# Attention, a feed-forward layer and routed experts in one kernel: another first expert, fewer static rows, a count in place of a flush, one state step

## The chip, the cores and the metric

The kernel runs on 1 core of one Trainium2 chip. The metric is the device time of one execution in microseconds (us), the median of several runs. The inputs are those of the reference below; weights w_in and w_out of the second layer arrive as 64-bit floats, all else as 32-bit floats.

## The reference

Three layers follow one another on 4 x 768 = 3072 tokens.

```python
# 1: linear attention with decay, 8 heads of 48
for t in range(S):
    cur = np.einsum('bhd,bhe->bhde', u[None] * kt, vt)
    y[:, :, t] = np.einsum('bhd,bhde->bhe', rt, state + cur)
    state = w[None, :, :, None] * state + np.einsum('bhd,bhe->bhde', kt, vt)
# 2: 384 -> 1024 -> 384
h = x @ w_in
e = np.exp(h - h_max); sm = e / (np.sum(e, axis=-1, keepdims=True) + 1e-09)
solu = h * sm
ln = (solu - mu) / np.sqrt(var + 1e-06) * g_ln
x = ln @ w_out
# 3: each token goes to one of 8 experts
expert_idx = np.argmax(x @ w_gate, axis=1)
for e in range(E):
    mask = expert_idx == e
    h = np.maximum(x[mask] @ w1[e], 0.0)
    out[mask] = gate_w[mask, None] * (h @ w2[e])
```

## The kernel before, in words

**Tiles and stages.** Tokens go in 24 tiles of 128. Layer 1 runs a chunked form: a tile is one chunk of 128 steps, six tiles make a sequence, and a state of 48 x 48 for each head is carried from tile to tile. `update` (line 433) computes what a tile adds to the state, for two heads at a time, so that PSUM holds 128 x 96 blocks of which only the two diagonal quarters are wanted; `advance` (lines 437 to 444) writes these two quarters, partitions 0 to 63 and 64 to 127, into `state`, with one VectorE instruction each, adding the decayed state `sdec` (line 447, `state` times `wdec`; `wdec` is zero off the diagonal quarters). Layer 2 is `mm1` (line 474), the softmax and norm (lines 480 to 526), and `mm2` (line 559), whose last columns are the gate. Routing is `choose`, `rank`, `place` and `send` (lines 566 to 616): each token gets a row in the DRAM table `xs`, 3072 rows for each expert, by the running counts `cum`. Layer 3 reads the rows of one expert after another back (`gather`, line 739), turns them (`etrans`, 753), and multiplies with w1 (`emm1`, 772) and w2 (`emm2t`, 815, where the expert has more than 384 rows, else `emm2`, 797, in tiles of 128 rows). Every f32 product is three products of split parts (high by high, high by low, low by high).

**Static rows.** An expert's count is known only on the chip, while its matmuls have fixed sizes: `CAPS` gives the rows of the first expert, and of the others in falling order of their counts. Rows beyond the count hold a token number that the scatter at the end leaves out. In the kernel before the first expert is always expert 0, with 480 rows, in two parts of 256 and 224 that can start before the last tiles are routed. After the last tile `count` and `sort` (lines 632 to 642) order the other seven by count, and `who` (line 648) loads the number of each as a register of SyncE, by which its weights and rows are addressed. `judge` (line 662 on) raises a flag when a count is over its static rows or a guard on the inputs fails; then a general path computes everything again.

**Weights.** w_in comes in three pieces of 128 x 1024, w_out in four of 128 x 768. `to_f32` (line 158) turns the two words of each 64-bit number into one 32-bit float: ScalarE takes the absolute value of the high word (line 167), VectorE flushes numbers under a bound to zero (line 169) and puts the bits together in three instructions (172, 174, 176). `win_hi`, `win_lo` (188, 191) and `wout_g`, `wout_max`, `wout_hi`, `wout_lo` (202 to 253) follow. Products of `mm1` need all of w_in, those of `mm2` all of w_out.

**What sets the order.** Every step is an `op` with an engine, a cost, what it comes after, and a priority `first`, worked out from the constants `X`. `plan` (line 1057 on) goes through the steps as a list scheduler: of those that could start within `X["EPS"]` of the earliest, the one with the lowest priority is next. The result is the program order on every engine, SyncE's DMA queue and GpSimd's queue among them. Some steps (`either`) go to VectorE or GpSimd, whichever the plan finds free first. The changed lines of the plan are in `conv` (873), the steps of layer 1 (931 on), `count` and `sort`, and the loop over the experts (about 980 on).

Of the kernel before, what the change touches and what calls it, by code (L numbers as in the profile page):

```python
# [8 lines left out]
F32 = mybir.dt.float32  # L9
F32R = mybir.dt.float32r  # L10
I32 = mybir.dt.int32
F16 = mybir.dt.float16
# [18 lines left out]
CAPS = (CAP, 480, 448, 432, 416, 400, 384, 368)  # L31
# [9 lines left out]
def body(ctx, tc, r, k, v, w, u, w_in, w_out, g_ln, w_gate, w1, w2, out):  # L41
# [18 lines left out]
    def sml(name, slot=None):  # L60
# [25 lines left out]
    X = dict(ET=-429.78, GG=-233.7, SO=-294.91, FL=-505.75, OL=1, ybuf=10, tmp=1, rkv=3, LAT=0.06, SELF=0.05,  # L86
             PRE=1.4, EPS=0.06, TA=144.7, TB=237.7, TM=276.51, NA=8, NB=9, M0=1038.64, W0=81.15, TW=251.26,
             W1=-298.48, TV=171.34, PF=134.77, PW=224.32, F0=466.45, EL=3, e=3, S0=12.3, P0=10.1, D0=2.5,
             L0=140.96, L1=105.03, U0=108.15, KG=5.83, PT=2, ZT=-610.22, F2=261, TE=288.64, GA=-152.99,
             GW=-226.57, GN=-97.54, DB=-0.71, KS=5.09, K0=202.89, K1=-109.3, xtrans=-983.06, kev=-515.9,  # L90
             ahi=-247.51, vlo=-135.95, ruk=1202.87, attend=-89.6, choose=-323.29, xhi=-244.14, vhi=27.84,
             own=138.51, hvar=-317, hmax=-289.95, gexp=-194.8, ktrans=655.01, rtrans=830.4, hexp=357.44,
             ztrans=-337.98, asum=-344.06, rev=-225.55, xlo=-713.89, decay=439.69, alo=897.3, rank=107.2,
             ld=344.13, xrow=-508.46, mm2=767.79, causal=-1488.31, hseed=638.5, send=114.58, hsolu=83.6,
             yout=-62.13, zlo=360.17, scores=-213.79, square=539.99, place=100.24, ysquare=-70.93,
             advance=-563.07, update=-90.68, zscale=-828, hroot=-416.04, mm1=19.74, aval=-17.98, kpow=98.58)
# [36 lines left out]
    G.memset(state, 0.0)  # L133

# [23 lines left out]
    def to_f32(t, n, is64, dst):  # L158

        dst.append(t[:, 0:n])  # L160
        if is64:
# [21 lines left out]
    def win_bits(c):  # L183
        raw["f", c] = f = []
        return to_f32(raw.pop(("i", c)), FF, w_in.dtype != F32, f)
# [10 lines left out]
    def wout_bits(c):  # L196
        raw["g", c] = f = []
        return to_f32(raw.pop(("o", c)), 2 * DM, w_out.dtype != F32, f)
# [56 lines left out]
    def fold_all():  # L255

        fold_load()
        for c in range(KD):
            win_load(c)
            run(win_bits, c)  # L260
            win_hi(c)
            win_lo(c)
        for c in range(0, KF, 2):
            wout_load(c)
            run(wout_bits, c)
# [13 lines left out]
    def tables():  # L279
# [4 lines left out]
        V.tensor_copy(wbad, wc)  # L284
        V.tensor_scalar(wc, wc, WLO, WHI, op0=ALU.max, op1=ALU.min)
        V.tensor_tensor(wbad, wbad, wc, op=ALU.not_equal)
# [342 lines left out]
    for e in range(1, E):  # L629
        V.memset(kcap[:, e:e + 1], 8.0 * CAPS[e] + 7)  # L630
# [704 lines left out]
```

## Time and profile before

| what | us |
|---|---|
| median of 3 runs | 634.06 |
| the runs | 633.23 to 634.15 |
| the profiled execution, its own time | 634.09 |
| its span, first to last instruction | 632.4 |
| PE (matmul) busy in the span | 578.8 |
| DVE (VectorE) busy | 455.9 |
| ACT (ScalarE) busy | 347.9 |
| POOL (GpSimd) busy | 272.0 |

The profile is that of one execution. Engines are PE for TensorE's matmuls, PEld for its weight loads, DVE, ACT, POOL and SP (SyncE, which issues most DMAs). Start times are counted from the first instruction. A group of instructions is named by its line, its engine, its operation, and what it writes and reads; "x24" is a count. A share of busy time over the whole span is a mean over stages that differ, so the stages are read one by one.

### The profile page before, as it was taken

The numbers are of one execution on the slowest core, as the hardware profiler recorded it, in microseconds if no ns is written. First come the engines' busy times: TensorE is split into PE (matmuls) and PEld (weight loads), VectorE is DVE, ScalarE is ACT, GpSimd is POOL, SyncE is SP. The second block draws the span as 40 slices with busy tenths as digits, with TensorE's granted clock in tenths as the row PEclk, the third lists the DMA queues.
The fourth block names the chain that finished last, engine by engine and source line by source line (L and its number), as shares of the span: only waits on it lengthen the run. The fifth ranks groups of instructions, "written<-read, shape, count | busy, mean of one in ns | idle before, by whom it ended". The sixth has DMA issues, their size and how long they took to land.

```text
span 632.4 us, 10941 instructions
## 1 busy us (share of the span) xinstructions
PE 578.8 (92%) x4037; PEld 497.1 (79%) x4037; DVE 455.9 (72%) x799; ACT 347.9 (55%) x577; POOL 272.0 (43%) x435
## 2 busy tenths in 40 slices
PE   2767887999999999999999989999999999999992
PEld 2667776867777777778877648998889999999992
DVE  7999989998798888888875655447665767578010
ACT  2754557379777676777756753445252535345210
POOL 3778767746755865665535452110001021001211
PEclk9876978999999999999999989999999999999997
DMA  9943736994565592947044624735455675764110
GB/s 170 227 109 60 157 93 198 238 160 93 99 116 95 106 129 54 154 72 129 28 76 98 196 100 163 273 107 189 129 182 161 200 203 170 208 141 108 52 38 23
DMA packets 163185, 83.79 MB, mean 132 GB/s; under 512 B 140100, under 2 KB 156346, under 8 KB 162736
## 3 DMA queue, kind: packets, MB, share of 16 engines
q1 hardware_dynamic: 159808, 73.51, 51.7%
q0 software_dynamic: 3312, 9.47, 4.5%
q8 instruction: 34, 0.56, 0.4%
q14 instruction: 31, 0.25, 0.1%
HBM read 51.71 MB, written 16.30 MB: 108 GB/s over the span
## 4 chain that ended last, share of the span: by engine, by line
PE 52%; DVE 17%; issue 10%; DMA 10%; POOL 4%; ACT 4%; POOLq 0%; SPq 0%; ACTq 0%; DVEq 0%
PE emm L772 12%; PE mm L559 10%; PE mm L474 9%; DMA out<-o,gt 8%; PE emm L815 7%; PE emm L797 3%; PE scores L396 2%; PE update L433 2%; DVE AT L400 2%; PE attend L419 2%; DVE tmp L169 2%; DVE tmp L174 2%; PE etrans L753 1%; DVE vl L369 1%; PE attend L422 1%
## 5 line engine op out<-in xcount | busy, mean ns | idle before, releaser
L847 POOL DMA_INDIRECT out<-o,gt x30 | 30.1, 1003 | 206.8 <-ACT o L843 104.3
L559 PE MATMUL mm<-wo,zT 128*128 128x392 f16 x576 | 100.7, 332 | 0.5 <-DVE zT L550 0.4
L474 PE MATMUL mm<-wi,xh 128*128 128x512 f32 x288 | 91.8, 400 | 3.3 <-DVE AT L400 3.3
L559 PEld LDWEIGHTS <-zT 128*128 128x128 f16 x576 | 55.9, 98 | 38.4 <-issue 1.3
L783 ACT ACTIVATE hh<-emm 128x896 fp32r<-128x896 f32 (+7 forms) x32 | 28.2, 882 | 82.3 <-PE emm L772 79.6
L786 DVE SCALAR_TENSOR_TENSOR hl<-emm,hh 128x896 fp32r<-128x896 f32 (+7 forms) x32 | 33.4, 1044 | 55.2 <-ACT hh L783 55.2
L772 PE MATMUL emm<-exh,w1h 128*128 128x256 f32 (+8 forms) x216 | 73.1, 338 | 0.0
L772 PE MATMUL emm<-exh,w1l 128*128 128x256 f32 (+8 forms) x216 | 72.6, 336 | 0.0
L772 PE MATMUL emm<-exl,w1h 128*128 128x256 f32 (+8 forms) x216 | 72.6, 336 | 0.0
L474 PEld LDWEIGHTS mm<-wi,xh 128*128 128x128 f32 x288 | 52.7, 189 | 13.6 <-DVE AT L400 3.7
L474 PE MATMUL mm<-wi,xl 128*128 128x512 f32 x144 | 56.5, 392 | 0.0
L815 PE MATMUL emm<-hh,w2h 128*128 128x480 f32 (+4 forms) x120 | 43.8, 365 | 0.0
L815 PE MATMUL emm<-hh,w2l 128*128 128x480 f32 (+4 forms) x120 | 43.1, 359 | 0.0
L815 PE MATMUL emm<-hl,w2h 128*128 128x480 f32 (+4 forms) x120 | 43.1, 359 | 0.0
L613 POOL DMA_INDIRECT xs<-row,pos x24 | 29.7, 1236 | 30.0 <-issue 13.8
L396 PE MATMUL scores<-rT,kT 64*128 64x128 f32 x384 | 32.5, 317 | 11.0 <-DVE st L494 7.7
L772 PEld LDWEIGHTS emm<-exh,w1l 128*128 128x128 f32 x216 | 40.7, 189 | 1.4
L772 PEld LDWEIGHTS emm<-exh,w1h 128*128 128x128 f32 x216 | 40.8, 189 | 1.4
L772 PEld LDWEIGHTS emm<-exl,w1h 128*128 128x128 f32 x216 | 40.8, 189 | 1.3
L396 PEld LDWEIGHTS scores<-rT,kT 64*128 64x128 f32 x384 | 27.4, 216 | 15.4 <-issue 7.0
L500 ACT ACTIVATE z<-e,st 128x1024 f16<-128x1024 f32 x24 | 27.5, 1145 | 18.0 <-DVE st L494 11.0
L480 DVE TENSOR_REDUCE st<-mm 128x1 f32<-128x1024 f32 x24 | 29.3, 1220 | 10.6 <-PE mm L474 9.2
(208 smaller groups left out, 1566.0 us busy)
## 6 DMA issues: line engine op xcount, KB each, us to landing
stage<-in_moe_w SPq DMA_DIRECT2D x16, 768.0 KB, 4.8
stage<-in_moe_w SPq DMA_DIRECT2D x8, 1024.0 KB, 5.0
xs<-zf SPq DMA_DIRECT2D x8, 772.0 KB, 12.2
rkv<-in_r SPq DMA_DIRECT2D x24, 192.0 KB, 4.9
rkv<-in_k SPq DMA_DIRECT2D x24, 192.0 KB, 5.1
rkv<-in_v SPq DMA_DIRECT2D x24, 192.0 KB, 4.5
stage<-in_moe_w SPq DMA_DIRECT2D x8, 512.0 KB, 4.2
xg<-xs SPq DMA_DIRECT2D x5, 772.0 KB, 6.4
```

The lines of the kernel that those rows point to most:

```text
L396: T.matmul(ps[:, a, j * P:(j + 1) * P], kT[h, j, :], rT[h, j, :], start=True, stop=True)
L474: T.matmul(ps[:, n, :], a[:, j, :], wi[b][:, j, n * 512:(n + 1) * 512], start=(j == 0 and m == 0), stop=(j == KD - 1 and m == 2))
L480: V.tensor_reduce(st[:, 0:1], tk["h", i], op=ALU.max, axis=AX.X, negate=True)
L500: A.activation(z[:, 0, :], tk["e", i], AF.Square, scale=-float(FF), bias=st[:, 2:3], accum_out=st[:, 4:5])
L559: T.matmul(ps[:, 0:OW], zz[:, a, c, :], wo[b][:, c, :], start=(c == 0 and m == 0), stop=(c == KF - 1 and m == 2))
L613: G.indirect_dma_start(out=xs, out_offset=bass.IndirectOffsetOnAxis(ap=pos.bitcast(U32), axis=0), in_=row, in_offset=None, bounds_check=E ...
L772: T.matmul(ps[:, x, :], a[:, j, fc * P:(fc + 1) * P], b[:, j, :], start=(j == 0 and m == 0), stop=(j == KD - 1 and m == 2))
L783: A.activation(cols(d, "hh", q), d["pm", q], AF.Relu)
L786: V.scalar_tensor_tensor(cols(d, "hl", q), d.pop(("pm", q)), 0.0, cols(d, "hh", q).bitcast(F32), op0=ALU.max, op1=ALU.subtract)
L797: T.matmul(ps[0:n, 0:DM], a[:, c, j * P:j * P + n], b[:, c, :], start=(c == 0 and m == 0), stop=(c == KF - 1 and m == 2))
L815: T.matmul(ps[:, 0:d["nr"]], a[:, c, m * P:(m + 1) * P], b[:, c, :], start=(c == 0 and x == 0), stop=(c == KF - 1 and x == 2))
L847: G.indirect_dma_start(out=out, out_offset=bass.IndirectOffsetOnAxis(ap=d["gt"][0:n, j, 1:2].bitcast(U32), axis=0), in_=d.pop(("o", j))[0: ...
```

## The change

1. The first expert is chosen on the chip: after tile 14 (`PK`) a matmul counts, `sort` and `leader` find the expert with the highest count, and `who(0)` loads its number on SyncE. Its weights and its gather wait for that. The sort at the end puts it first by adding 1e6 to its key.
2. `CAPS` falls for the other seven: 120 rows fewer in all. `judge` checks the first expert by its mask `first8`.
3. `to_f32` flushes nothing any more. ScalarE computes, after the absolute value, how far each word lies below the bound, and sums that into a column of `wbad`; any such word raises the flag. VectorE's three bit instructions read the high words in place.
4. `advance` writes the whole 128 x 384 block with one instruction. The off-diagonal quarters of `state` now hold numbers, and `wdec` makes them zero in `sdec`.
5. The constants `X` of the plan are others, and the costs of the changed steps in the plan too.

```diff
-CAPS = (CAP, 480, 448, 432, 416, 400, 384, 368)
+CAPS = (CAP, 464, 432, 416, 400, 384, 368, 344)
...
-    X = dict(ET=-429.78, GG=-233.7, SO=-294.91, FL=-505.75, OL=1, ybuf=10, tmp=1, rkv=3, LAT=0.06, SELF=0.05,
-             PRE=1.4, EPS=0.06, TA=144.7, TB=237.7, TM=276.51, NA=8, NB=9, M0=1038.64, W0=81.15, TW=251.26,
...
+    X = dict(PK=14, ET=-29.23, GG=-120.46, SO=-383.87, FL=374.6, OL=1, ybuf=10, tmp=1, rkv=3, LAT=0.06,
+             SELF=0.05, PRE=1.4, EPS=0.1, TA=176.56, TB=248.64, TM=254.17, NA=8, NB=9, M0=495.42, W0=42.93,
...
-    cuma = const.tile([P, 1], F16, name="cuma")
+    cuma = const.tile([P, E], F16, name="cuma")
...
-    wbad = const.tile([P, 4], F32, name="wbad")
+    wbad = const.tile([P, 12], F32, name="wbad")
+    thr = const.tile([P, 1], F32, name="thr")
...
+    G.memset(wbad, 0.0)
+    G.memset(thr, 1.125 * 2.0 ** -15)
...
             A.activation(hm.bitcast(F32), hi.bitcast(F32), AF.Abs)
             yield
-            V.scalar_tensor_tensor(hm.bitcast(F32), hm.bitcast(F32), 1.125 * 2.0 ** -15, hi.bitcast(F32),
-                                   op0=ALU.is_ge, op1=ALU.mult)
+            if small is None:
+                V.scalar_tensor_tensor(hm.bitcast(F32), hm.bitcast(F32), 1.125 * 2.0 ** -15, hi.bitcast(F32),
+                                       op0=ALU.is_ge, op1=ALU.mult)
+                hi = hm
+            else:
+                A.activation(hm.bitcast(F32), hm.bitcast(F32), AF.Relu, scale=-1.0, bias=thr, accum_out=small)
             yield
-            V.tensor_scalar(a, hm, 3, 0x3FFFFFF8, op0=ALU.logical_shift_left, op1=ALU.bitwise_and)
+            V.tensor_scalar(a, hi, 3, 0x3FFFFFF8, op0=ALU.logical_shift_left, op1=ALU.bitwise_and)
             yield
-            V.scalar_tensor_tensor(a, hm, -0x40000000, a, op0=ALU.bitwise_and, op1=ALU.bitwise_or)
+            V.scalar_tensor_tensor(a, hi, -0x40000000, a, op0=ALU.bitwise_and, op1=ALU.bitwise_or)
...
     def advance(i):
-        p4 = tk.pop(("pu", i))[:, 0:DM].rearrange("p (j a d) -> p j a d", j=4, a=2)
-        for a in range(2):
-            h = slice(64 * a, 64 * a + 64)
-            if i % NC == 0:
-                V.tensor_scalar(state[h, :, a, :], p4[h, :, a, :], SV, None, op0=ALU.mult)
-            else:
-                V.scalar_tensor_tensor(state[h, :, a, :], p4[h, :, a, :], SV, sdec[h, :, a, :], op0=ALU.mult, op1=ALU.add)
+
+        flat, ps = state.rearrange("p j a d -> p (j a d)"), tk.pop(("pu", i))[:, 0:DM]
+        if i % NC == 0:
+            V.tensor_scalar(flat, ps, SV, None, op0=ALU.mult)
+        else:
+            V.scalar_tensor_tensor(flat, ps, SV, sdec.rearrange("p j a d -> p (j a d)"), op0=ALU.mult, op1=ALU.add)
...
+    def leader():
+
+        V.tensor_scalar(first8, iota8, lead[:, 0:1], None, op0=ALU.is_equal)
+        yield
+        V.scalar_tensor_tensor(koff, first8, 1e6, koff, op0=ALU.mult, op1=ALU.add)
...
     def who(e):
 
-        which[e] = nc.values_load(perm[0:1, e:e + 1].bitcast(I32), engines=[mybir.EngineType.SP], min_val=1, max_val=E - 1)
+        src = perm if e else lead
+        which[e] = nc.values_load(src[0:1, e:e + 1].bitcast(I32), engines=[mybir.EngineType.SP], min_val=0, max_val=E - 1)
...
-        V.tensor_scalar(over[:, 0:1], ps[:, 2 * NT:2 * NT + 1], float(CAP), None, op0=ALU.is_gt)
         V.tensor_reduce(fl[:, 1:2], over, op=ALU.max, axis=AX.X)
-        V.tensor_scalar(fl[:, 4:5], ps[:, 2 * NT:2 * NT + 1], float(2 * P), None, op0=ALU.min)
-        V.tensor_tensor(fl[:, 4:5], fl[:, 4:5], ps[:, 2 * NT + E:2 * NT + E + 1], op=ALU.is_gt)
+
+        V.tensor_tensor(over, ps[:, 2 * NT:2 * NT + E], eoff, op=ALU.subtract)
+        V.tensor_tensor(keys, ps[:, 2 * NT + E:2 * NT + 2 * E], eoff, op=ALU.subtract)
+        V.tensor_scalar(over, over, float(2 * P), None, op0=ALU.min)
+        V.tensor_tensor(over, over, keys, op=ALU.is_gt)
+        V.tensor_tensor(over, over, first8, op=ALU.mult)
+        V.tensor_reduce(fl[:, 4:5], over, op=ALU.max, axis=AX.X)
...
-        op(("bits", kind, c), "", [("act", 1.15 * t), ("dve", 1.4 * t), ("dve", 1.3 * t), ("dve", 1.4 * t), ("dve", 1.4 * t)] if F64 else [("dve", .01)],
+        op(("bits", kind, c), "", [("act", 1.15 * t), ("act", 1.15 * t), ("dve", 1.1 * t), ("dve", 1.4 * t), ("dve", 1.4 * t)] if F64 else [("dve", .01)],
...
-            op(("advance", i), "dve", .71, [("update", i), ("decay", i - 1), ("decay", i - 2)], advance, i, first=f + X["advance"])
+            op(("advance", i), "dve", .55, [("update", i), ("decay", i - 1), ("decay", i - 2)], advance, i, first=f + X["advance"])
...
+    PK = X["PK"]
+    op("pick", "pe", .06, [("place", PK)], count, bank="s", until=[("picked", 0)], first=0)
+    op("picked", "", [("dve", .25), ("dve", .18), ("dve", .27)], ["pick"], lambda: sort(lead), first=0)
+    op("leader", "", [("dve", .25), ("dve", .17)], ["picked"], leader, first=0)
+    ops[("place", PK + 1), 1]["after"].append("pick")
+    for x in (("sort", 0),):
+        ops[x]["after"].append("leader")
+    op(("who", 0), "dma", .5, ["leader"], who, 0, first=0)
...
-                op(("wload", e, n), "dma", m * w_ * 4 * P / 230e3, [("yout", NT - 1)] + [("who", e), ("wlo", e, n - 2) if n > 1 else ("wlo", e - 1, n + 2), ("wload", e, n - 1) if n else ("wload", e - 1, 3)],
+                op(("wload", e, n), "dma", m * w_ * 4 * P / 230e3, [("yout", NT - 1), ("who", 0)] + [("who", e), ("wlo", e, n - 2) if n > 1 else ("wlo", e - 1, n + 2), ("wload", e, n - 1) if n else ("wload", e - 1, 3)],
```

## Rows read from the trace of the kernel before

**Rows 1.** The page, part 2: busy tenths in 40 slices of the span.
```profile
PE   2767887999999999999999989999999999999992
DVE  7999989998798888888875655447665767578010
```

**Rows 2.** Stretches: length; PE, PEld, DVE, ACT, POOL busy us (instructions); clock; DMA.
```profile
20.00:125.00 105.00, 82.76 (x727) 74.50 (x727) 100.47 (x122) 61.44 (x104) 79.47 (x66) 0.85 0.66 150
125.00:360.00 235.00, 231.25 (x1823) 178.40 (x1822) 193.70 (x401) 170.43 (x301) 139.15 (x285) 1.00 0.59 105
360.00:382.00 22.00, 17.99 (x109) 10.55 (x107) 11.44 (x40) 13.45 (x25) 11.79 (x30) 0.92 0.35 118
382.00:620.30 238.30, 238.04 (x1339) 226.68 (x1338) 134.25 (x181) 95.20 (x136) 31.71 (x36) 1.00 0.51 154
```

**Rows 3.** The chain of waits in order of time: start, us, what.
```profile
28.54 3.07 DVE tmp L169
...
151.04 3.98 PE mm L559 x24
```

**Rows 4.** Stretches, line 772 alone: experts' first products at 224, 480, 448, 368 rows.
```profile
401.50:409.70 8.20, 8.17 (x72) 1.00 0.91 310
418.00:433.80 15.80, 15.74 (x72) 1.00 0.31 102
...
451.60:466.30 14.70, 14.70 (x72) 1.00 0.62 161
...
595.70:607.80 12.10, 12.10 (x72) 1.00 0.13 48
```

**Rows 5.** The same for second products: line 815 at 480 and 448, line 797.
```profile
435.70:451.60 15.90, 15.83 (x72) 1.00 0.46 155
468.20:483.00 14.80, 14.80 (x72) 1.00 0.59 201
...
582.90:595.70 12.80, 12.73 (x72) 1.00 0.13 47
```

**Rows 6.** The same for the transposes, line 753: four tiles, three tiles.
```profile
418.00:435.70 17.70, 1.91 (x12) 1.00 0.36 121
...
555.40:556.50 1.10, 1.00 (x9) 1.00 1.02 227
```

**Rows 7.** Groups by line and form, DVE: xcount, busy us, mean ns, idle before.
```profile
L169 DVE SCALAR_TENSOR_TENSOR tmp<-tmp,raw 128x1024 f32<-128x1024 f32 x3 | 5.6, 1876 | 0.0
...
L169 DVE SCALAR_TENSOR_TENSOR tmp<-tmp,raw 128x768 f32<-128x768 f32 x4 | 5.4, 1360 | 0.1
```

**Rows 8.** Lines 169 and 172: ns min/median/max, first and last start.
```profile
L169 DVE SCALAR_TENSOR_TENSOR tmp<-tmp,raw x7: 949/1256/3149, 9.8 to 107.1; 128x768 f32<-128x768 f32 x4, 128x1024 f32<-128x1024 f32 x3
...
L172 DVE TENSOR_SCALAR tmp<-tmp x7: 545/1022/2321, 11.0 to 108.4; 128x768 int32<-128x768 int32 x4, 128x1024 int32<-128x1024 int32 x3
```

**Rows 9.** Timeline of POOL around 28 us: start, us, instruction.
```profile
28.09 2.44 POOL L409 TENSOR_TENSOR al<-AT,ah 128x1024 f16<-128x1024 f32 x1
```

**Rows 10.** Timeline of DVE near the start.
```profile
9.77 1.22 DVE L169 SCALAR_TENSOR_TENSOR tmp<-tmp,raw 128x1024 f32<-128x1024 f32 x1
```

**Rows 11.** Lines 167 and 344 on ACT: ns min/median/max, first and last start.
```profile
L167 ACT ACTIVATE tmp<-raw x7: 891/920/1143, 8.4 to 105.8; 128x768 f32<-128x768 f32 x4, 128x1024 f32<-128x1024 f32 x3
...
L344 ACT ACTIVATION_READ_ACCUMULATOR sq<-rkv x24: 185/189/211, 14.2 to 301.7; 128x1 f32 x24
```

**Rows 12.** Stretch with line 444 alone, DVE busy; and line 427's group.
```profile
0.00:125.00 125.00, 4.91 (x14) 0.88 0.72 157
...
L427 DVE SCALAR_TENSOR_TENSOR av<-attend,av 128x384 f32<-128x384 f32 x24 | 13.2, 552 | 2.3 <-PE attend L422 1.4 <-PE rank L593 0.7
```

**Rows 13.** Timeline of DVE: the place of tile 14.
```profile
306.04 0.17 DVE L597 CUSTOM_DVE_ANT_0 mx<-rank,oh 128x8 f32<-128x8 f32 x1
```

**Rows 14.** SP: the first expert's first weight loads; the register loads of line 648.
```profile
346.31 1.04 SPq L700 DMA_DIRECT2D stage<-in_moe_w  x2
...
L648 SPq TENSOR_LOAD <-perm x7: 263/273/530, 385.4 to 392.4; - x7
```

More of the change, by code (lines that the diff above doesn't have):

```diff
@@ L156, in raw_load, with to_f32 @@
         return t
-    def to_f32(t, n, is64, dst):
+    def to_f32(t, n, is64, dst, small):
         dst.append(t[:, 0:n])
@@ L181, in win_load, with win_bits @@
         raw["i", c] = raw_load(w_in, c, 1)
-    def win_bits(c):
+    def win_bits(c, count=True):
         raw["f", c] = f = []
-        return to_f32(raw.pop(("i", c)), FF, w_in.dtype != F32, f)
+        return to_f32(raw.pop(("i", c)), FF, w_in.dtype != F32, f, wbad[:, 4 + c:5 + c] if count else None)
     def win_hi(c):
@@ L194, in wout_load, with wout_bits @@
         raw["o", c] = raw_load(w_out, c, 2)
-    def wout_bits(c):
+    def wout_bits(c, count=True):
         raw["g", c] = f = []
-        return to_f32(raw.pop(("o", c)), 2 * DM, w_out.dtype != F32, f)
+        return to_f32(raw.pop(("o", c)), 2 * DM, w_out.dtype != F32, f, wbad[:, 8 + c // 2:9 + c // 2] if count else None)
     def wout_g(c):
@@ L259, in fold_all @@
             win_load(c)
-            run(win_bits, c)
+            run(win_bits, c, False)
             win_hi(c)
@@ L264, in fold_all @@
             wout_load(c)
-            run(wout_bits, c)
+            run(wout_bits, c, False)
             wout_g(c)
@@ L621, in body @@
     V.tensor_scalar(eoff, iota8, float(N), None, op0=ALU.mult)
-    koff, kcap, keys = (const.tile([P, E], F32, name=n) for n in ("koff", "kcap", "keys"))
-    perm = const.tile([P, E], U32, name="perm")
+    koff, kcap, keys, first8 = (const.tile([P, E], F32, name=n) for n in ("koff", "kcap", "keys", "first8"))
+    perm, lead = (const.tile([P, E], U32, name=n) for n in ("perm", "lead"))
     V.tensor_scalar(koff, iota8, -8.0 * N - 1, 7.0, op0=ALU.mult, op1=ALU.add)
-    V.memset(koff[:, 0:1], 1e6)
-    V.memset(kcap[:, 0:1], 1e7)
-    for e in range(1, E):
-        V.memset(kcap[:, e:e + 1], 8.0 * CAPS[e] + 7)
+    for e in range(E):
+        V.memset(kcap[:, e:e + 1], 8.0 * CAPS[e] + 7 + (0 if e else 1e6))
     def count(slot):
@@ L659, in flags @@
         T.matmul(ps[:, 2 * NT:2 * NT + E], ones16, cum, start=True, stop=True)
-        T.matmul(ps[:, 2 * NT + E:2 * NT + E + 1], ones16, cuma, start=True, stop=True)
+        T.matmul(ps[:, 2 * NT + E:2 * NT + 2 * E], ones16, cuma, start=True, stop=True)
     def judge():
@@ L970, in body @@
     b_left = set(ops)
-    last = [(n, i) for n in ("place", "ysquare", "square", "causal") for i in range(NT)]
+    last = [("bits", "i", c) for c in range(KD)] + [("bits", "o", c) for c in range(0, KF, 2)] + [(n, i) for n in ("place", "ysquare", "square", "causal") for i in range(NT)]
     op("count", "pe", .06, [("place", i) for i in range(NT)], count, bank="s", until=[("sort", 0)], first=X["SO"])
@@ L1005, in body @@
         nq, nx = (4, 2) if wide else (2, 4)
-        op(("gath", y), "dma", 3.4 * kt if wide else 1.7, (sent + [("who", e)] + [("etr", y - 2 if wide else y - 1, x) for x in range(KD)] + [("tail", y - 2)] if y else [("send", LT)]),
+        op(("gath", y), "dma", 3.4 * kt if wide else 1.7, (sent + [("who", e)] + [("etr", y - 2 if wide else y - 1, x) for x in range(KD)] + [("tail", y - 2)] if y else [("send", LT), ("who", 0)]),
            lambda d=d, e=e, r0=r0, nr=nr, nt=nt: (d.update(part(ep if e else e0, e, r0, nr, nt * P if e else nr)), gather(d)), first=f - X["GA"] * (y > 1) + X["GG"] * (y > 1))
```

31 lines of the change are left out of this document (16 added, 15 removed).

## The prediction

> **What bounds the kernel now.** I read the page's 40 slices first [rows 1]: DVE stands at 9 and 8 tenths over the first eight to ten slices, while PE starts at 2, climbs unevenly, and stands at 9 from the tenth slice on but for one dip. So the span has a ramp that DVE fills and a long rest that PE fills. The view of engine time by stretches then puts numbers on it [rows 2]. [...] From 125 to 360 us PE is busy 231.25 of 235 at full clock and DVE 193.70. From 360 to 382 us, where the last tokens are routed, PE leaves 4.0 us idle. From 382 to 620.3 us, the experts, PE is busy 238.04 of 238.30. Last, the chain of waits in order of time says the same from the other side [rows 3]: in the ramp it is made of DVE's pieces, among them one line 169 of 3.07 us, and later of whole products of PE, one after another (lines 559 and 474). Hence two rules for pricing: time taken off PE in the expert stage is worth its full amount, time taken off DVE is worth something in the ramp alone, and ACT, POOL and SP cost something only where their cover ends.
>
> **The rows fewer.** The static rows of experts 1 to 7 go from 480, 448, 432, 416, 400, 384, 368 to 464, 432, 416, 400, 384, 368, 344. Five sizes stand in both lists, so the change is: the passes of 480 and 448 go, passes of 464 and 344 come. A first product (72 matmuls) took 15.74 us at 480 rows, 14.70 at 448, 12.10 at 368 and 8.17 at 224 [rows 4]; at 464 it should take the mean of the first two, 15.22. For 344 I have bounds: on the slope from 480 to 368 (0.0325 us a row) 11.3, on that from 368 to 224 (0.0273) 11.45; I take 11.4, near both. So 15.74 + 14.70 - 15.22 - 11.4 = 3.8 us. The second product of an expert over 384 rows streams its rows (15.83 at 480, 14.80 at 448), and one of three tiles streams 384 columns for each tile whatever the rows: 12.73 us [rows 5]. 344 rows are three tiles, so 15.83 + 14.80 - 15.32 - 12.73 = 2.6 us. One expert with four tiles becomes one with three, and its transposes go from 1.91 to 1.00 us [rows 6]: 0.9 us. Together **7.3 us**, all on PE while it has no gap. What could hide it is a weight or gather that comes too late for shorter passes; DVE is busy 134 and ACT 95 of these 238 us [rows 2], so the splits have room.
>
> **The words counted instead of flushed.** Line 169, one DVE instruction for each of the seven weight pieces, goes. By its groups it was busy 5.6 + 5.4 = 11.0 us [rows 7], all of it between 9.8 and 108 us. But its shortest pass is 0.95 us, its longest 3.15 [rows 8]. The longest is the one at 28.5 us in the chain [rows 3], and it begins inside a tensor operation of POOL that itself takes 2.44 us [rows 9]; line 172 shows the same spread [rows 8]. Unstretched, seven passes are 4 x 0.95 + 3 x 1.22 (the 1,024 wide one at 9.8 us) [rows 10] = 7.5 us. What the other 3.5 us were, waiting for POOL, the next DVE instruction would meet in its place; I take **7.5** and keep 11.0 as the other end.
>
> [...]
>
> Line 172 now reads every second word of the raw piece. Line 169 read the same words at 0.95 us for 768, so a stride has no price of its own there; line 172's shortest pass, 0.545 us, is at a faster rate, and it could lose that. Its median is 1.02 us already, against 1.06 for a mean pass at the slow rate, so I take 0; the ends are 0 and 7 x 0.45 = 3.2 us more (0.45 is the mean 1.06 at the slow rate less the 0.6 or so of the fast one). ACT gets the count: seven passes like its absolute value, 4 x 0.92 + 3 x 1.14, and seven readings of the accumulator at 0.19 [rows 11], 8.4 us. ACT idles 43.6 of the ramp's 105 us, which covers it; without the cover 8.4 us would go straight against the gain. The words test no longer stands before the three shifts, so the chain of a piece gets shorter, not longer. The count is read at the very end of the routing, 270 us later: free.
>
> **The state's step.** Two halves of 0.35 us become one of the size of line 427 (128 x 384 from PSUM with a second operand), 0.55 [rows 12]: 0.15 us for each of 20 tiles. Before 125 us line 444 ran 14 times, for seven tiles; these are tiles 1 to 4 and 7 to 9 (the last tile of a sequence takes no step), so tiles 0 and 6, which open a sequence and go through line 442, lie there too. Nine tiles make **1.4 us** of DVE. The other eleven lie under PE in the stretch that PE fills and are worth nothing; should PE run out of work there they would give 1.6 us.
>
> **The leader.** After tile 14 (15 tiles) come one small matmul, five small DVE instructions and one register load on SP. In the old order that tile's place is found at 306 us [rows 13]. The DVE work is about 5 x 0.17 us under a PE that is full; the load, like the seven of line 648, is 0.53 us at worst [rows 14]. On SP's queue, token loads and the transposes of z stand behind it; if SP reaches it before the counts are there, these wait, and after them the second products. The first expert's weights, which also wait for the last attention tile, were loaded from 346 us on [rows 14], 40 us later, so the new dependency is met long before. With no cover all of this is 5 x 0.17 + 0.53 = 1.4 us. The judgement gets three such DVE instructions more, with the first expert's first product running on PE beside them: 0, at most 0.5. The clearing of the twelve flag words on POOL lies at the start, before the first wait of DVE for the table of w: 0.
>
> **The sum.** The DVE saving of the ramp is 7.5 + 1.4 = 8.9 us; DVE fills 96% of that stretch, and from its end PE is full, so I pass 0.96 of it on: 8.5. The new priorities of the planner also reorder everything; a trace of the old order gives that no value. I take 0, and as ends 4.0 us either way, the idle time of PE in the routing stretch [rows 2]. The profiled execution took 634.09 us, 1.7 more than its span, and the median is 634.06, the same. 634.1 - 7.3 - 8.5 = **618.3 us**.
>
> **The rivals.**
> *The ramp gives nothing* (0.25): what DVE sheds is taken up by POOL, busy 79.47 of the 105 us [rows 2], or by the longer queue on ACT, and PE starts as late as before. For it: POOL's 2.44 us operation [rows 9] is one on which the attention waits. Against it: DVE idles 4.5 us there and POOL 25.5. 634.1 - 7.3 = 626.8 us.
> *The ramp gives more* (0.15): the whole 11.0 + 1.4 us comes back, with 4.0 from the order, as PE's clock of 0.85 would rise with fewer gaps. 634.1 - 7.3 - 16.4 = 610.4 us.
> *Slower* (0.07): the new order lets the w_out pieces fall behind the attention tiles, so that second products start later. PE then idles in the ramp, where it already leaves 22.2 us [rows 2]. It decides from a delay of 15.8 us if the DVE saving stands, of 7.3 if it is eaten; with that idle time doubled and the saving eaten, 634.1 - 7.3 + 22.2 = 649 us. Against it: DVE has less to do for each piece.
> *The change trips its own guards* (0.01): then the general path runs, whose price no row has, far over the range. By the reference with its first seed the counts are 318, 370, 422, 415, 400, 392, 308, 447; the leader after 15 tiles is expert 2 with 422 (480 static), and 447, 415, 400, 392, 370, 318, 308 lie within the seven new sizes.
>
> **How the numbers follow.** 0.50 for the forecast of 618.3, the rest as above, with 0.02 left for a balance near zero. The low end is the third case, 610.4; the high end is the second with 1.4 us of uncovered small work on top, 628.2. Outside I leave about 0.15: the slower cases and the half of the third case that lies beyond its middle. About 0.2% is what a measurement can tell from no change. Faster: 0.50 + 0.25 + 0.15 = 0.90; same 0.02; slower 0.07 + 0.01 = 0.08.
>
> **What would show it.** The expert stage from first product to last shorter by 7.3 us with PE still without gaps; no product of 448 or 480 columns left. Line 169 gone, its successors at the same mean; and the stretch in which PE is full at clock 1.00 begins some 8 us earlier than 125 us; lines 442 and 444 are one pass of 0.55 us each. I am wrong on the ramp if DVE is still full to 125 us, on the experts if PE shows gaps there, and on the leader if SP's queue waits on the register load while PE stands.

## The result, and the profile after

The changed kernel took 626.27 us (median of 13 runs, 624.37 to 632.68), the kernel before 634.43 us beside it (13 runs, 633.23 to 635.24): a ratio of 0.9885, 95% interval 0.9862 to 0.9908. By the medians 8.2 us were gained, by the ratio 7.3 (634.43 x 0.0115; its interval gives 5.8 to 8.8), where 15.8 were forecast. Two of the thirteen runs took 632.20 and 632.68 us, at a mean granted clock of 0.953 against 0.965 to 0.970 in the others.

Two rows of the page first, the busy tenths in 40 slices, which answer to [rows 1].

```profile
PE   0757798999999999999999989999999999999990
DVE  5899989978898989989877653537576767546211
```

PE stands at 9 from the eighth slice on, as it did before (the prediction read "from the tenth" off [rows 1]); what went is the dip to 8 in the 24th. So the tenths show no shorter ramp. The first slice of PE went from 2 to 0 and that of DVE from 7 to 5: the kernel starts later. The engine time by stretches says how much, and answers to [rows 2] (columns as there; the stretches are cut at the first product of the experts, 377.6 us, and at 610.3, where the last is about to end).

```profile
0.00:20.00 20.00, 4.85 (x21) 4.11 (x22) 11.13 (x51) 5.71 (x9) 4.32 (x18) 1.00 0.92 187
20.00:125.00 105.00, 83.18 (x690) 69.85 (x689) 97.99 (x125) 68.74 (x115) 70.40 (x64) 0.87 0.65 149
125.00:360.00 235.00, 235.00 (x1903) 183.09 (x1902) 197.10 (x401) 176.02 (x311) 136.49 (x286) 1.00 0.59 112
360.00:377.60 17.60, 14.03 (x94) 8.61 (x92) 9.40 (x32) 10.16 (x21) 9.65 (x25) 1.00 0.18 61
377.60:610.30 232.70, 231.40 (x1333) 222.44 (x1333) 124.73 (x160) 93.59 (x135) 36.17 (x35) 1.00 0.52 153
610.30:624.90 14.60, 0.34 (x5) 0.25 (x4) 2.19 (x15) 0.58 (x1) 1.02 (x1) 0.58 0.05 13
```

From 125 to 360 us PE now has no gap at all (235.00 of 235; 231.25 before). Cut into three parts, with the end of the span as the tail, the two profiled executions compare like this (us; the first part ends where the first matmul of the experts' first product starts, the second where the last second product ends):

| | front | expert stage | tail | span |
|---|---|---|---|---|
| before | 382.3 | 238.3 | 11.8 | 632.4 |
| after | 377.6 | 232.9 | 14.5 | 624.9 |

The front gave 4.7 us where 8.5 were forecast, the stage 5.4 where 7.3 were, and the tail, which was forecast to stay, took 2.7.

**The expert stage.** The sizes came as priced: this is the first-product line (789 now) alone, in the passes of 464, 368 and 344 rows.

```profile
415.00:430.20 15.20, 15.18 (x72) 13.44 (x72) 1.00 0.60 208
559.30:573.80 14.50, 12.86 (x72) 12.04 (x72) 1.00 0.35 121
586.30:597.80 11.50, 11.50 (x72) 11.30 (x71) 1.00 0.07 25
```

464 rows took 15.18 us and 344 rows 11.50 (15.22 and 11.4 were worked out); the second product at 344 rows took 12.67, as one of three tiles did before [rows 5]. The pass of 368 rows spreads over 14.5 us, 12.10 before [rows 4]: some transposes lie in it, and the only wait of PE over 0.1 us after the stage's start is this one, for ScalarE's output tile, for which ScalarE itself had waited 2.78 us until a scatter ended:

```profile
PE etrans L770 <- ACT o L820: 1.3, 1, 1.3
```

**The start.** The first matmul waits for the table made from w, 14.5 us into the span (9.2 before, the first line here). VectorE's timeline behind it shows why; under that is ScalarE's first row.

```profile
9.23 1.09 PE L311 MATMUL tables<-ident,rT 128*128 128x128 f32 x4 [9.23 <-DVE rT L305]
```

```profile
6.03 0.10 DVE L302 TENSOR_TENSOR tt<-tt 128x4 f32<-128x4 f32 x1
10.62 0.56 DVE L378 SCALAR_TENSOR_TENSOR vl<-rkv,vh 128x384 f16<-128x384 f32 x1 [4.48 <-ACT vh L374]
11.09 0.16 DVE L302 TENSOR_TENSOR tt<-tt 128x4 f32<-128x4 f32 x1
...
13.68 0.68 DVE L314 TENSOR_TENSOR rT<-tt 128x512 f32<-128x512 f32 x1
```

```profile
7.62 1.28 ACT L353 ACT_TABLE_LOAD   x1 [7.62 <-DMA rkv<-in_v]
```

The instructions of the table are issued ahead of the planned ones, but the first planned ones that wait for nothing of the table slip in between. Here it is `vl`, which waits 4.48 us for ScalarE, and ScalarE waits for the transfer of a token tile; the rest of the table stands behind it on VectorE.

**The tail.** The judgement used to end at 388.1 us (the first line, of the kernel before). The constant `FL` went from -505.75 to 374.6, and now the flags are the last product and the judgement follows it (the timeline; then line 1208, the branch on the flag, on TensorE's sequencer).

```profile
387.97 0.15 DVE L675 CAST fli<-fl 128x1 int32<-128x1 f32 x1
```

```profile
610.29 0.32 PE L671 MATMUL flags<-guard,mask 128*128 128x48 f32 x2
610.68 0.18 DVE L677 COPY guard<-flags 128x24 f32<-128x24 f32 x1 [11.10 <-PE flags L673]
...
613.07 0.15 DVE L692 CAST fli<-fl 128x1 int32<-128x1 f32 x1
```

```profile
L1208 PEldq COMPARE_BRANCH  x1: 3876/3876/3876, 613.9 to 613.9; - x1
```

### The profile page after: what moved, and what is told of

Its sections match the earlier page's. It is cut to its first block, busy times and chain, and to the rows that moved or that the text cites. A ratio compares the mean times of both kernels' runs of the same rounds, so it can differ in the third digit from the quotient of the medians.

```text
span 624.9 us, 10949 instructions
## 1 busy us (share of the span) xinstructions
PE 568.8 (91%) x4035; PEld 488.3 (78%) x4035; DVE 442.5 (71%) x781; ACT 354.8 (57%) x590; POOL 258.0 (41%) x427
## 5 line engine op out<-in xcount | busy, mean ns | idle before, releaser
L864 POOL DMA_INDIRECT out<-o,gt x29 | 34.5, 1190 | 196.4 <-ACT o L860 84.1
L800 ACT ACTIVATE hh<-emm 128x928 fp32r<-128x928 f32 (+8 forms) x32 | 27.6, 861 | 69.5 <-PE emm L789 58.1
L482 PEld LDWEIGHTS mm<-wi,xh 128*128 128x128 f32 x288 | 54.2, 194 | 11.4 <-DVE AT L409 0.8
L803 DVE SCALAR_TENSOR_TENSOR hl<-emm,hh 128x928 fp32r<-128x928 f32 (+8 forms) x32 | 32.4, 1011 | 32.0 <-ACT hh L800 31.9
L726 DVE TENSOR_TENSOR w2l<-stage,w2h 128x768 fp32r<-128x768 f32 x32 | 30.1, 952 | 18.2 <-ACT w2h L724 18.2
L726 DVE TENSOR_TENSOR w1l<-stage,w1h 128x1024 fp32r<-128x1024 f32 x24 | 28.9, 1221 | 13.0 <-ACT w1h L724 13.0
L528 ACT ACTIVATE e<-e,st 128x1024 f32<-128x1024 f32 x22 | 27.3, 1239 | 16.4 <-POOL st L524 16.4
L428 PE MATMUL attend<-sdec,rT 128*128 128x96 f32 x160 | 35.4, 307 | 0.0
L814 PE MATMUL emm<-w2h,hh 128*128 128x384 f32 (+3 forms) x104 | 35.2, 339 | 0.0
L814 PE MATMUL emm<-w2h,hl 128*128 128x384 f32 (+3 forms) x104 | 35.0, 337 | 0.0
L814 PE MATMUL emm<-w2l,hh 128*128 128x384 f32 (+3 forms) x104 | 35.0, 336 | 0.0
```

What stands on the lines that cost most here:

```text
L428: T.matmul(ps[:, j * 96:j * 96 + 96], rT[:, j, :], sdec[:, j].rearrange("p a d -> p (a d)"), start=True, stop=False, skip_group_check=True)
L482: T.matmul(ps[:, n, :], a[:, j, :], wi[b][:, j, n * 512:(n + 1) * 512], start=(j == 0 and m == 0), stop=(j == KD - 1 and m == 2))
L528: A.activation(e, e, AF.Identity, scale=st[:, 10:11], bias=st[:, 11:12])
L726: V.tensor_tensor(lo, d[:, x], hi.bitcast(F32), op=ALU.subtract)
L800: A.activation(cols(d, "hh", q), d["pm", q], AF.Relu)
L803: V.scalar_tensor_tensor(cols(d, "hl", q), d.pop(("pm", q)), 0.0, cols(d, "hh", q).bitcast(F32), op0=ALU.max, op1=ALU.subtract)
```

## The experiments

Each ran beside the kernel before, which had medians of 633.89 to 634.21 us in its four sets of runs, on three chips; a ratio is always to the kernel before of the same set. Front, stage and tail are cut as above, in the one profiled execution of each run. Line numbers are those of the run's own kernel (line 181 of the changed kernel is 180 in some of them).

**The order undone.** The changed kernel with the constants X of the kernel before (and `PK=14`); all else as changed.

```diff
-    X = dict(PK=14, ET=-29.23, GG=-120.46, ...
+    X = dict(PK=14, ET=-429.78, GG=-233.7, ...
```

> The changed code with the order constants X of the kernel before (PK=14 added). Theory (the code is worth the forecast 15.8 us, the new order gave half of it back: 5 us at the start, 2 us by mixing the experts' products, 2.5 us by a judgement that stands last): the judgement and the experts' products go back to their old places, but the three bit instructions no longer wait for ScalarE and now stand among the table's, so the start still loses about 4 us: 622 to 624 us. Rival (what VectorE sheds in the ramp is worth nothing, the order is no cause): 626 to 628 us, with the expert stage 7 us shorter than before and the first expert product at 382 us as before.

635.76 us, ratio 1.0032 (1.0017 to 1.0046): slower than before, and neither expectation. The first matmul waited until 15.6 us, here behind line 180 of the first piece, which no longer waits for ScalarE, stood fourteenth on VectorE with only memsets ahead of it, and waited 6.5 us for its transfer. So a part of both versions was lost at the start, which had to go before the rest could be read.

**The judgement early again.**

```diff
-             FL=374.6
+             FL=-505.75
```

> The changed kernel with one constant, FL, at its old value, so that flags and judge run beside the first expert's product again. Theory: the stretch from the last product to the end falls from 14.6 to 12.1 us, 626.3 - 2.5 = 623.8 us. Rival (the last scatter's landing and its waits set the end anyway): 626.3 us, the stretch still 14 us or more.

626.52 us, 0.9874 (0.9855 to 0.9894). The tail was 12.1 us, as the theory had it and not the rival, but the stage took 235.3, 2.4 more, and the total is the rival's number. The trace shows where the 2.4 us are: PE's one wait in the stage, for ScalarE's output tile as above, grew from 1.3 to 2.2 us, and from 565 to 570 us, right behind it, the granted clock was 0.67, where the changed kernel had 1.00 after its wait. Why that wait grew stays open; with other constants the early judgement cost nothing (below).

**The table ahead.** `tables()` is issued within the planned order, as its first step, so nothing can slip in; once with the constants of the change, once with those of before.

```diff
-    tables()
...
     man.__enter__()
+    tables()
```

> The changed kernel with the table of w computed ahead of all planned steps on every engine, so that no planned VectorE step stands among its instructions. Theory: the table is ready at about 9 instead of 14.3 us, and the whole ramp starts some 4 to 5 us earlier: first expert product at 373 instead of 377.6 us, 621 to 622 us in all. Rival (the ramp waits for transfers or for GpSimd, so an earlier table is worth nothing): 626 us.

621.29 us, 0.9795 (0.9774 to 0.9817), the theory: the first matmul came at 8.1 us, the first expert product at 372.1, 5.5 earlier than in the changed kernel, with stage (233.0) and tail (14.5) the same. The start is settled, and this version beats both kernels.

> The changed code, the order constants of the kernel before, and the table of w ahead of all planned steps. Theory (the code is worth the forecast once the order takes nothing back): 617 to 620 us, first expert product near 374 us, expert stage 231 us. Rival (what VectorE sheds in the ramp is worth nothing): 626 to 628 us, first expert product near 382 us.

630.52 us, 0.9949 (0.9929 to 0.9968), again neither. The stage was 230.9, so the rows are worth 7.4 us, as forecast; but the front was 383.9, later than before, with less work on VectorE. The ramp was worth less than nothing in this order.

**The saving alone, in the order of before.** The words, and then words and step, in the kernel before (table ahead), with its plan and the plan's costs untouched: every engine keeps its program order, and only these instructions change. The base is the kernel before with the table ahead.

```diff
-            V.scalar_tensor_tensor(hm.bitcast(F32), hm.bitcast(F32), 1.125 * 2.0 ** -15, hi.bitcast(F32), ...
+                A.activation(hm.bitcast(F32), hm.bitcast(F32), AF.Relu, scale=-1.0, bias=thr, accum_out=small)
...
+            V.scalar_tensor_tensor(flat, ps, SV, sdec.rearrange("p j a d -> p (j a d)"), op0=ALU.mult, op1=ALU.add)
```

> The kernel before with its table of w issued inside the planned order, ahead of it; nothing else. It is the base for the next two, whose orders are the same as its own. In the kernel before the table already stands ahead of the first piece of w_in on VectorE, so both theories expect 633 to 635 us, as before, and a first product of the experts at 382 to 383 us.

> The base with the counted words only: no line 169 on VectorE, a sum on ScalarE in its place. The plan and its costs are those of the kernel before, so every engine keeps its program order and only these seven instructions change. Theory A (the saving is real as long as the order stays, and in the old order with new costs it was the re-planning that gave it away): the ramp gets shorter by 7.5 x 0.96 = 7.2 us, so 626 to 628 us with the first expert product near 375 us. Theory B (VectorE is full in the ramp, yet tensor products there wait on other things as long, the clock and the chain of attention tiles among them): under 2 us, so 632 to 634 us with the first expert product at 380 us or later.

> As the run with the counted words, and the state's step as one instruction too, again in the program order of the kernel before. Theory A: 1.4 us less than the counted words alone, 625 to 627 us. Theory B: within 0.7 us of the counted words alone, 631 to 634 us.

The base took 635.04 us, the words 627.69, words and step 627.26 (ratios to before 1.0014, 1.0000 to 1.0028; 0.9902, 0.9879 to 0.9924; 0.9889, 0.9865 to 0.9913). Theory A: 7.35 us for the words where 7.2 were forecast, though by the two intervals anything from about 5.5 to 9 us; another 0.4 for the step, less than these runs resolve. The profiled execution of the words is one of its slower ones (630.53 us): in the traces the front goes from 382.7 us to 378.0 with the words and 375.5 with the step too. The stretch from 100 to 125 us shows it, base above, words below:

```profile
100.00:125.00 25.00, 21.87 (x191) 19.75 (x192) 24.78 (x33) 13.76 (x24) 20.66 (x21) 0.93 1.01 257
```

```profile
100.00:125.00 25.00, 25.00 (x224) 22.83 (x223) 24.05 (x41) 14.27 (x26) 19.38 (x19) 0.92 1.11 263
```

PE is now full from 100 to 125 us, under a VectorE that is nearly as full as before.

**All of the change in the order of before.** Leader, rows, words and step, the table ahead, old constants, and the plan's costs of pieces and step put back too.

```diff
-        op(("bits", kind, c), "", [("act", 1.15 * t), ("act", 1.15 * t), ("dve", 1.1 * t), ...
+        op(("bits", kind, c), "", [("act", 1.15 * t), ("dve", 1.4 * t), ("dve", 1.3 * t), ...
-            op(("advance", i), "dve", .55, ...
+            op(("advance", i), "dve", .71, ...
```

> Everything the change does in its instructions (leader, rows fewer, counted words, one state step), the table of w ahead, but the plan's constants X and the plan's costs of the pieces and of the state step as in the kernel before. The products stand in the order of the kernel before up to the counting after tile 14. Theory A (the saving is real where the order stays): the first expert product at 375.5 us as with words and state alone, the expert stage 230.8, the tail 13: a span near 619.5 and 620 to 622 us. Rival D (the leader's steps or the shorter experts take it back): 624 to 628 us, with the first expert product at 380 us or later.

620.2 us, 0.9789 (0.9759 to 0.9818): theory A, 13.7 us less than before against the 15.8 forecast. (Its six runs fall into two groups, 617.66 to 618.73 and 621.66 to 622.76; the profiled one is of the lower.) Front 373.3, stage 231.1, tail 12.7; from 100 to 125 us PE is full at full clock:

```profile
100.00:125.00 25.00, 25.00 (x213) 22.46 (x211) 24.65 (x41) 14.25 (x25) 16.11 (x16) 1.00 1.10 241
```

So between this kernel and the one of 630.52 us stand two costs in the plan and nothing else; the intervals of the two ratios lie apart.

**The order alone, with the old work.** The kernel before, table ahead, once with the changed kernel's costs under the old constants, once with its constants under the old costs.

> The kernel before with the table ahead, its instructions unchanged; only the plan's costs are those of the changed kernel (two steps of ScalarE and three of VectorE for a piece, 0.55 for the state's step), with the old constants. So the old work stands in another order. Theory A (re-planning with new costs under constants that were fitted to the old ones is what took 8 us in the run of the old order): 640 to 645 us, the first expert product at 388 to 393 us. Rival: that order is bad for the new work only, and the old work takes 633 to 636 us in it.

> The kernel before with the constants X of the changed kernel and the table of w ahead: the new order alone, with the old costs, the old instructions and the old rows. Theory (new order and saved work add up; with all the work changed the new order's first expert product came at 372.1 us, 3.4 us earlier than 375.5 in the old order): 379 us for the first expert product, and with an expert stage that loses 2 us to its mixing and 2 us of tail, 634 to 637 us. Rival 1 (the order does most of the front's gain by itself): first expert product at 374 us or earlier, 629 to 632 us. Rival 2 (the constants fit the new costs alone): first expert product at 386 us or later, 642 us or more.

642.84 us (1.0137, 1.0115 to 1.016) and 644.44 us (1.0187, 1.0162 to 1.0212): 7.8 and 9.4 us more than the base's 635.04 for nothing but another plan: the turn of the steps, and for the `either` steps the engine. Fronts 390.3 and 388.5. The first hit theory A, the second rival 2: the new constants do not serve the old costs. Their stretches from 100 to 125 us, in that order:

```profile
100.00:125.00 25.00, 22.76 (x170) 20.24 (x170) 23.84 (x36) 12.62 (x23) 16.45 (x16) 0.84 1.09 247
```

```profile
100.00:125.00 25.00, 25.00 (x163) 20.87 (x163) 20.01 (x36) 14.27 (x25) 8.34 (x13) 0.85 1.08 224
```

PE is busy here for 22.76 and 25.00 us, but at a granted clock of 0.84 and 0.85, where the base has 0.93. The second lost its time earlier: from 20 to 100 us its PE is busy for 55.87 us at 0.76, the base's for 61.13 at 0.85.

**Which cost, and what it does.** The whole change with old constants: one of the two costs new at a time, then both new with the low parts of the scores (line 417) of ten tiles held on GpSimd.

```diff
-        op(("alo", i), "either", (2.25, 1.3), ...
+        op(("alo", i), *(("pool", 2.25) if i < 10 else ("either", (2.25, 1.3))), ...
```

> As the run of the whole change under the old constants and old costs (620.2 us), but the state's step is planned at 0.55 instead of 0.71. Theory E (the pieces' planned costs move the order, the step's do not): 619 to 622 us. Rival F (any cost that is planned lower lets a step that may go to either engine slip onto VectorE; in this order three low parts of the scores stand on VectorE ahead of the last piece, where the kept order has none): 626 to 631 us.

> The same with the pieces planned at their new costs and the step at its old 0.71. In this order two low parts of the scores stand on VectorE ahead of the last piece. Theory E: 628 to 632 us, as with both costs new (630.5). Rival F: the same, 626 to 631 us; E and F part in the run before this one. If neither cost by itself does it: 619 to 622 us.

> The whole change under the old constants with both new costs, as in the run that took 630.5 us, except that the low parts of the scores of tiles 0 to 9 (line 417) are held on GpSimd, as the kept order has them; the planner may no longer put them on VectorE. Theory G (the loss is the choice of engine: VectorE, the fuller one in the ramp, gets GpSimd's work): 620 to 625 us, with PE full from 100 us on. Rival H (it is the turn of the steps, pieces ahead of attention tiles, whichever engine makes the low parts): 628 to 632 us.

629.13, 637.78 and 630.11 us (0.9917, 1.0053, 0.9939), fronts 383.4, 393.4 and 384.1. The second's twelve runs fall into two groups, 633.46 to 635.85 and 639.71 to 641.83 us; its median lies between them, and its front is that of the upper. Theory E falls: the step's cost alone, 0.71 to 0.55, loses 9 us. Rival F has the number of the first run and not of the second. Theory G falls for line 417: it had moved in the ramp, as the two lines' views show, the kept order above, both costs new below,

```profile
L417 POOL TENSOR_TENSOR al<-AT,ah x10: 2130/2386/2867, 22.3 to 114.3; 128x1024 f16<-128x1024 f32 x10
```

```profile
L417 POOL TENSOR_TENSOR al<-AT,ah x6: 2131/2295/2896, 30.2 to 105.2; 128x1024 f16<-128x1024 f32 x6
L417 DVE TENSOR_TENSOR al<-AT,ah x2: 1550/1783/2016, 25.3 to 52.7; 128x1024 f16<-128x1024 f32 x2
```

but holding it on GpSimd gave nothing back. What the rows do show is that by 125 us the kept order has made ten tiles' low parts and the other eight, with the last weight piece done at 106.6 and 102.0 us: there the pieces got ahead of the attention tiles, and PE went short (22.70 of 25 us busy from 100 to 125 us). But with the step's cost alone new the last piece ends at 118.1 us, later than in the kept order, and PE has 20.56 there at a clock of 0.73; so no one shift is common to the orders that lose. Rival H, the turn of the steps, has the number of the last run, but it is not shown: only line 417 was held there, and over the whole trace 16 other `either` steps still stand on VectorE that the kept order has on GpSimd (7 of `kp`, 4 of `av`, 3 of `sdec`, 2 of `ru`). Whether their engine or the turn of the steps costs the time stays open, and so does which step costs most.

**The constants of the experts.** The changed kernel with the table ahead and the eleven constants of experts and judgement as before; then the same with the scatter of an output tile planned at 6.0 us.

```diff
-             ET=-29.23, GG=-120.46, SO=-383.87, FL=374.6, F0=-386.07, F2=148.59, TE=84.91, ...
+             ET=-429.78, GG=-233.7, SO=-294.91, FL=-505.75, F0=466.45, F2=261, TE=288.64, ...
```

> The changed kernel with the table of w ahead of the plan, and the eleven constants that place the experts, their loads and the judgement put back to those of the kernel before (ET, GG, SO, FL, F0, F2, TE, GA, GW, GN, PW). Up to the first expert product the products stand in the order of the version with the table ahead alone (372.1 us, 621.3 in all); from there on no expert's second product is mixed into the next one's first product. Theory C (the expert stage lost 2 us to that mixing and the tail 2 us to the late judgement): 372.1 + 230.7 + 13 and 1.7 around it, 617 to 618.5 us, with the flags' products in the first expert's first product. Rival: the stage is set by when weights and gathers come after the new front, and the mixing only fills their waits: 620 to 622 us with waits of PE between experts.

618.79 us, 0.977 (0.9753 to 0.9788), between the two expectations. It is the lowest median of all; against the changed kernel's 0.9885 the intervals lie apart, against the table ahead alone (0.9795) and the whole change in the old order (0.9789) they overlap. Front 372.0 as expected, tail 12.1 where 13 was, but the stage still 232.8 with no product mixed into another: that half of theory C falls. The 1.8 us more than in the old order sit at the pass of 368 rows again, here as the wait of PE and ScalarE's timeline show:

```profile
PE emm L788 <- DVE hl L802: 1.2, 1, 1.2
```

```profile
552.63 0.58 ACT L819 ACTIVATE o<-emm,gt 128x384 f32<-128x384 f32 x1 [4.43 <-DMA out<-o,gt]
557.47 0.59 ACT L819 ACTIVATE o<-emm,gt 128x384 f32<-128x384 f32 x1 [4.26 <-DMA out<-o,gt]
557.95 0.84 ACT L724 ACTIVATE w2h<-stage 128x768 fp32r<-128x768 f32 x1
558.68 0.78 ACT L799 ACTIVATE hh<-emm 128x736 fp32r<-128x736 f32 x1
```

ScalarE waits for a scatter to free an output buffer, and the split `hh` that the product's buffer waits for is queued behind it.

> The version with the new front and the old experts' constants (618.8 us), with one figure of its plan changed: the scatter of an output tile is planned at 6.0 us instead of 2.4, so that ScalarE takes the next expert's splits ahead of output tiles whose buffer is not free yet. Theory: in the version before this, ScalarE waited 4.4 us for the scatter's end with the splits of the first product of 368 rows behind it, and that product took 13.92 us where 12.08 was seen; this goes, so 616.5 to 617.5 us. Rival: the output tiles come later and the tail grows as much: 618.5 to 620 us.

619.72 us, 0.9783 (0.976 to 0.9806): the rival's number, not its mechanism, as the tail went from 12.1 us to 12.4 only. The pass of 368 rows took 12.16 us, as the theory had it, but the second product behind it waited 1.4 us for a split that now came later, and the stage stayed at 232.7: the wait moved. A fifth output buffer was not tried.

## Why the prediction was right, and where it was wrong

**The bounds** were read rightly in the main: PE is busy for 231.40 of 232.70 us in the stage, with one gap of 1.3. The slices were misread (above), without an effect on the sum, and one sign was badly chosen: "wrong on the ramp if DVE is still full to 125 us". DVE is busy for 24.05 and 24.65 of the 25 us up to 125 in the two runs that show the ramp's gain, and the gain is there.

**The rows fewer** held. 7.3 us were worked out; with the old constants the stage went from 238.3 to 230.9 and 231.1, 7.4 and 7.2 less. (With the late start of the first experiment it took 232.4: PE had no gap there, but a granted clock of 0.73 over its first 6.3 us.) Under the new constants it is 5.4 less, for one queue on ScalarE; the prediction had named a split or a gather that comes too late, and it let ACT's 95 busy us of 238 [rows 2] rule that out. An average says nothing of one wait of 2.8 to 4.4 us in program order.

**The ramp** held as well, in the order of the kernel before: 7.35 us for the words against 7.2. That it agrees to 0.15 us is luck, by the width of the runs and by the steps to it. In the pair of traces with one order the flush took 11.3 us (5.8 + 5.4; 11.0 in [rows 7]), 3.8 more than its shortest passes. The prediction let such a stretch (3.5 us by its rows) come back on "the next DVE instruction", and so it did, but not on the three lines of bits, which went from 26.55 to 24.46 us: the ten passes of `vl` ahead of the last piece went from 11.4 to 15.4. Up to the last piece VectorE's other instructions, the same in both runs, took 3.8 us more, three at the very start left out, which shift the table of w by 0.2 us only. So 11.3 + 2.1 - 3.8 = 9.6 us of VectorE's time went, not 7.5, and less of it was passed on than 0.96: 4.7 us between the two traces, 7.35 between the medians. Where the stretch comes from the traces show as well (below): from GpSimd, inside whose operations 60 of 119 passes began in five traces. The strided read of line 181 had the right price, 0: its passes of 768 words took 547 ns on the mean, as the shortest of line 172 [rows 8].

**The state's step** was sized right, in the line's view of the changed kernel:

```profile
L452 DVE SCALAR_TENSOR_TENSOR state<-update,sdec x16: 536/544/558, 30.3 to 320.6; 128x384 f32<-128x384 f32 x16
```

Its 1.4 us can't be told from 0.4 by the runs.

**The leader** was free, as forecast. SP did wait for it,

```profile
SPq L661 <- DVE first L652: 7.0, 1, 7.0
```

but PE is full in that stretch (8.00 of 8 us from 295 to 303), and the sign named for being wrong needed both.

**The judgement** was wrong: "0, at most 0.5", with the first expert's first product beside it. The diff moved `FL`, and with it the judgement behind the last product; there it costs 2.4 us of tail (14.5 against 12.1 with the other expert constants and the same front).

**The order** is the step that failed: "I take 0, and as ends 4.0 us either way". What it cost is the changed kernel less the whole change in the old order, with its table ahead: 6.1 us by the medians (626.27 - 620.2), of the 8.0 by which the forecast was missed, and by the spans of the two profiled executions 624.9 - 617.0 = 7.9 us: 4.3 of front (the start takes 5.5, the new order gives 1.2), 1.8 of stage, 1.8 of tail. So a term put at 0 measured 6 to 8 us, beyond its own end.

The measured prices of an order are wider still: 7.8 and 9.4 us with the old work, 8.9 (620.2 to 629.13), 10.3 (to 630.52) and 17.6 (to 637.78; 14 to 20 by its two groups) with the new. Of the two halves of the edit, with the table ahead, the costs lost those 10.3 us and the constants won back 9.2 (630.52 to 621.29); that the balance is near the 0 that was taken is luck. What is left is the start, the late judgement and ScalarE's queue, which came with them. The end of 4.0 us had been read from the idle time of PE in one stretch, which bounds what an order can gain there and not what it can lose. Two of the three could be seen beforehand: the diff shows `FL`, by which the judgement goes, and the kernel shows that `tables()` stands ahead of the plan and so has no place in it.

**The rivals.** "The ramp gives nothing" has the number, 626.8, but not the mechanism: POOL was busy less, 70.40 us for 79.47 [rows 2], and the front came 4.7 us earlier. "The ramp gives more" had PE's clock rise with fewer gaps, which the runs do not show: from 100 to 125 us PE was busy for all 25.00 us at 0.85, 0.92 and 1.00 in three of them. "Slower" had the w_out pieces fall behind; in the changed kernel the last piece ends at 99.1 us, at 114.3 before.

## What to carry to other kernels

Where a planner sets the program order, a change of its costs is a change of its own: time the edit first with the order held, then the order with the edit held, and give the order a term as wide as such runs show. A step put off to "where nobody waits" needs a look at who reads its result at the end, and a step issued outside the plan a look at what can slip in between. In the run with the old expert constants ScalarE, busy for 93.26 of 232.90 us, waited 4.43 and 4.26 us for scatters, and PE, busy for 231.60, then stood 1.2 us for a split queued behind the second of these waits: an engine that is mostly idle needs a look at what stands behind its waits.

## What the runs showed of the hardware

In five traces (the kernel before and after, and the runs of the base, of the words, and of the whole change in the old order) a VectorE pass over a weight piece that began while a `TENSOR_TENSOR` of GpSimd ran took its own time and, on top, what was left of that operation, less 0.12 to 0.13 us. This held for all 60 passes that began so; the other 59 took the shortest time of their form within 0.03 us. One of each, from the run of the words, in ns as line 180's shortest and longest:

```profile
L180 DVE TENSOR_SCALAR tmp<-raw x7: 550/682/2367, 10.3 to 104.9; 128x768 int32<-128x768 int32 x4, 128x1024 int32<-128x1024 int32 x3
```

The longest begins at 79.34 us, 0.18 into a GpSimd operation of 2.14 us (line 417), and ends at 81.71; the shortest, at 92.67, has no GpSimd operation beside it. [rows 9] shows the same: line 169 at 28.46 us, begun inside an operation that ends at 30.53.

TensorE's sequencer took 3.36 to 4.37 us in nine traces for the one branch at the end, where the other engines took 50 to 72 ns. With an early judgement it started ahead of the last product's end (before: flag read at 617.3, branch at 617.9, last product until 620.6):

```profile
L1183 PEldq COMPARE_BRANCH  x1: 3356/3356/3356, 617.9 to 617.9; - x1
```

With the late one it followed the last product and ended at 617.8 us, 7.3 behind it, and the other engines' closing waits stood behind it, at 617.9 to 618.9; GpSimd's began 7.4 us behind the last product, 5.1 in the run with the early judgement and the old expert constants. That is the 2.4 us. No run shows what the branch spends its time on.

ScalarE's table load of 1.28 us stood at 7.62 us in the changed kernel, at 0.80 us in the kernel before and with the table ahead, where nothing waited for it:

```profile
0.80 1.28 ACT L167 ACT_TABLE_LOAD   x1 [0.80 <-PEq L1322]
```

It is not that the first activation waits only in the first case: it waits in all three, in the kernel before 6.29 us for a transfer, with the table ahead 7.17 for TensorE, and there behind the load. What differs in the traces is a semaphore instruction of the same line, which in the changed kernel stands ahead of the load, at 7.55 us, and in the two others does not. At 7.62 us the load's 1.28 us lie in the chain that the first matmul waits for.
